# A scan and a mixture of adapters on one core: two gating subtractions bound to GpSimd, a later four-bank rotation, and one store cut into 112 and four times 4 rows

## The chip, the cores and the metric

The kernel runs on one core of a Trainium2 chip. The metric is the device time of one execution in microseconds (us), the median of several executions. A core has a TensorE (PE) for matmuls and transposes, a VectorE (DVE), a ScalarE (ACT), a GpSimd (POOL) and a SyncE (SP), each with its own instruction stream, and 16 DMA engines that move data between HBM and the on-chip memory (SBUF). Matmul results go to PSUM, which has eight banks. "PEld" in the profile is TensorE's weight load.

## The reference

```python
def _attn_ref(a, b):                       # a, b: (8, 6400, 128) float32
    h = np.zeros((B, D)); out = np.zeros_like(b)
    for t in range(S):
        h = a[:, t] * h + b[:, t]
        out[:, t] = h
    return out

def _moe_ref(x, w_gate, A, B):             # x: (51200, 128), E = 8 adapters, r = 16
    logits = x @ w_gate
    topk = np.argpartition(-logits, K, axis=1)[:, :K]        # K = 2
    sel = np.take_along_axis(logits, topk, axis=1)
    w = np.exp(sel - sel.max(-1, keepdims=True)); w /= w.sum(-1, keepdims=True) + 1e-09
    delta[mask] += w[mask, k, None] * (x[mask] @ A[e] @ B[e])   # for each adapter e, each of the two choices k
    return x + delta

def reference(**kw):
    out = _attn_ref(a, b)
    return _moe_ref(out.reshape(B * S, D), moe_w_gate, moe_A, moe_B)
```

A first-order recurrence runs along each of the 8 sequences. Its result x goes, row by row, through the two best of eight rank-16 adapters, weighted by a softmax of the two logits.

## The kernel before

**Units.** The 51,200 rows are cut into 100 units of 512 rows. For each unit w the inputs a and b are transposed on TensorE into PSUM (AB), ScalarE copies a out (aev), and VectorE runs the recurrence over the 512 columns (scan, line 520). It starts from the last column of the unit before, so the hundred scans form one chain. The result xT is float16 and lies in a ring of 16 units.

**What follows a scan.** For unit v TensorE computes the eight logits per row (L) and z = x·A for all adapters (Z). VectorE or GpSimd multiplies z by the gate weights (mul, line 739; units in POOL_MULS go to GpSimd by way of a ScalarE copy, zev, line 725). TensorE transposes the product (T), ScalarE copies it back (tev, line 796), and TensorE sums x (R) and the product times B (D) in a PSUM bank. That bank is copied into a slot of the 24-unit ring outt (oev, line 842), by ScalarE alone up to unit 89 and by ScalarE or VectorE from unit 90 on.

**Gating.** The units are put together in 29 groups, mostly of four. The last two are group 27 (units 93 to 96) and group 28 (units 97 to 99). The first three and the last two groups are "quick": VectorE sorts the eight logits of each row (mx, MAX8, line 599), then p4 (line 609) subtracts the second largest from all logits and p1 (line 618) the largest. From d2 and d1 follow p5 (line 670, a comparison), p6 (line 677, a sum), p7 (line 684, a sum) and the sigmoid on ScalarE (sig, line 694). In a quick group the planner may put each of p1, p4, p5, p6 and p7 on GpSimd or on VectorE. In the other groups they are all on GpSimd.

**Order.** A planner (`_Plan.schedule`) simulates the engines with costs in ns that are written into the source. Whenever an engine comes free it takes, of the operations that can start soonest there, the one with the smallest key. An operation that names two engines goes to the one where it can start first. The result is one fixed instruction order for each engine, with semaphore waits. All waits in an engine's stream are in that order, so whatever stands behind a waiting instruction waits too.

**PSUM banks for the sums.** Up to unit `OUT4 - 1` the sums R and D alternate between the two pO banks, and unit v waits for the copy-out of unit v-2. From unit OUT4 on four banks rotate: pO0, pO1, and the two pB banks that hold the transposed b until the last scans. There the first two units wait for the copy-outs two units back, the next two for scan 98 and scan 99, and all later ones for the copy-out four units back.

**Transfers.** All loads and stores of the big arrays are issued by SP, in the planner's order. Two units go together in one transfer of 128 rows of 4 KB. The first two and the last four units are stored alone, as 128 rows of 2 KB. `SPLIT` names stores that are issued in several pieces by rows: the pairs 66/67 and 72/73 are issued as 68 and 60 rows. Up to pair 68/69 a store also waits for the scan of a later unit (HOLD, FREE). From pair 70/71 on it waits for its copy-outs alone. The last load is issued at 160.20 us of the profiled execution, so from there on SP issues stores only.

Of the kernel before, what the change touches and what calls it, by code (L numbers as in the profile page):

```python
# [32 lines left out]
NOUT = 24  # L33
TAIL = 10
FILLS = 1
SPLIT = {66: (68, 60), 72: (68, 60)}
OUT4 = 86
LATE = {
    "sig": -205.0, "L": 9.0, "AB": -68.5, "zev": 29.9, "oev": -39.1, "tev": -12.4, "mul": -15.8, "aev": 52.7,
    "scan": 11.3, "T": 36.4, "R": 11.1,  # L40
# [60 lines left out]
class _Plan:  # L101
# [9 lines left out]
    def add(self, name, eng, kind, unit, cost, emit, deps=(), dma=None, bank=None, mode=None):  # L111

        engs = (eng,) if isinstance(eng, str) else eng
        cost = cost if isinstance(cost, dict) else {e: cost for e in engs}
        self.ops[name] = _Op(name, engs, kind, unit, cost, emit, list(deps), dma, bank, mode)
# [100 lines left out]
def bass_associative_scan_2x2__then__mixture_of_adapters_kernel(  # L216
# [18 lines left out]
    NU = N // UT  # L235
# [24 lines left out]
    with ExitStack() as stack:  # L260
# [299 lines left out]
        def gating(k):  # L560
            u0, n = groups[k]
# [3 lines left out]
            quick = k < QUICK[0] or k >= len(groups) - QUICK[1]  # L565
            ge = ("pool", "dve") if quick else "pool"
# [3 lines left out]
            def cost(t):  # L570
                p0, p1 = pool_cost[t]
                p, d = p0 + p1 * n, 160.0 + 27.0 * n
                return {"pool": (p, p + 85.0), "dve": (d - 75.0, d + 75.0)}
# [5 lines left out]
                return t[:, 0:c].to_broadcast([128, c, E])  # L579

            def step(name, eng, time, emit, deps):
                if isinstance(time, str):
                    time = cost(time)
                    time = {e: time[e] for e in ((ge,) if isinstance(ge, str) else ge)}
                add(f"{name}_{k}", eng, "gate", u, time, emit, deps)

            add(
# [14 lines left out]
            if quick:  # L602
                first, second = mx[s][:, 0:c, 0], mx[s][:, 0:c, 1]
                step("mx", "dve", (65.0 * c, 65.0 * c + 170.0), sort, [f"lev{k}", f"p1_{k - 2}", f"p4_{k - 2}"])
                step(
                    "p4",
                    ge,
# [4 lines left out]
                    [f"mx_{k}", f"p6_{k - 2}", f"p5_{k - 2}"],  # L612
                )
                step(
                    "p1",
                    ge,
# [187 lines left out]
        def o_bank(v):  # L804
            return pO[v % NO] if v < OUT4 else (pO + pB)[(v - OUT4) % 4]

        def o_free(v):
            if v < OUT4 + 2:
                return f"oev{v - NO}"
            return f"scan{NU - 2 + v % 2}" if v < OUT4 + 4 else f"oev{v - 4}"  # L810

# [49 lines left out]
        def store(j):  # L861
# [3 lines left out]
            slots = outt[:, s0 : s0 + n, :].rearrange("p n c -> p (n c)")  # L865
            sizes = SPLIT.get(u0, (128,))
            for k, size in enumerate(sizes):
# [84 lines left out]
```

## Time and profile before

| | us |
|---|---|
| median of 3 runs | 203.99 (203.7 to 204.33) |
| the profiled execution, its own time | 203.76 |
| its span, first to last instruction | 201.8 |
| TensorE busy | 190.8 (95%) |
| VectorE busy | 185.1 (92%) |
| ScalarE busy | 174.4 (86%) |
| GpSimd busy | 112.9 (56%) |
| granted TensorE clock | 0.996 |

All times inside the execution are counted from the start of the span. The profiled execution's own time is 1.96 us longer than its span, and 0.23 us shorter than the median.

How to read the profile: a row of a timeline is start, duration, engine, source line, operation, output<-input with partitions x elements, how many were merged into the row, and in square brackets the idle time before it and what ended that. A row of a table of stages gives for each engine the busy us and in brackets how many instructions fell in the stage, then the granted clock, the mean busy share of the 16 DMA engines and the GB/s they moved. A row of DMA issues gives output<-input, the issuing queue, how many, KB each, and the us from issue to landing, that is until the last of the 16 engines has finished its share. SPq is SP's queue of DMA issues.

### The profile page before, as it was taken

The page shows a single profiled execution, that of the slowest core. Times are in us where ns is not written, and L with a number is a line of the kernel's source. Part 1 is how long each engine was busy: PE and PEld are TensorE (multiplying, and loading weights), DVE is VectorE, ACT ScalarE, POOL GpSimd, SP SyncE. Part 2 cuts the span into 40 slices and gives each one's busy share as a digit, 9 for nine tenths or more (in the row PEclk, how much of TensorE's full clock was granted, in tenths as well). Part 3 has the DMA queues.
Part 4 walks back from the last instruction along what each step waited for, and adds up shares of the span by engine and source line. Part 5 has one row for each costly group of instructions (what it writes and reads, how often), then busy time and mean ns, then how long its engine had stood idle before and what let it go on. Part 6 is the DMA issues. An engine that isn't in the chain of part 4 may idle for free.

```text
span 201.8 us, 8755 instructions
## 1 busy us (share of the span) xinstructions
PE 190.8 (95%) x3594; PEld 171.3 (85%) x3594; DVE 185.1 (92%) x286; ACT 174.4 (86%) x381; POOL 112.9 (56%) x220
## 2 busy tenths in 40 slices
PE   7888989899999999999999999999999999999890
PEld 3667878798899999999999999999999998999890
DVE  1599999899999999999999999999999999999991
ACT  2367957978999999999999999999999998989991
POOL 1326577877386656746746665574675663556300
PEclk9999999999999999999999999999999999999998
DMA  6999999999999999999999999999999999998696
GB/s 180 403 409 404 410 403 406 407 403 412 406 413 413 410 413 417 409 413 411 411 411 417 409 415 410 410 415 413 409 414 413 410 413 412 411 376 338 262 374 246
DMA packets 23693, 79.35 MB, mean 393 GB/s; under 512 B 3686, under 2 KB 3814, under 8 KB 23654
## 3 DMA queue, kind: packets, MB, share of 16 engines
q1 hardware_dynamic: 22326, 78.65, 97.5%
q8 instruction: 29, 0.48, 0.9%
q10 hardware_dynamic: 1328, 0.14, 0.5%
q14 instruction: 10, 0.08, 0.1%
HBM read 52.56 MB, written 26.21 MB: 390 GB/s over the span
## 4 chain that ended last, share of the span: by engine, by line
PE 83%; DVE 8%; ACT 3%; issue 3%; POOL 1%; DVEq 0%
PE pA L95 27%; PE pO L91 21%; PE pTL L95 13%; PE pZ L91 10%; PE pTL L91 5%; DVE xT L520 5%; PE pB L95 3%; PE pB L91 3%; ACT a_st L501 2%; DVE mx L599 1%; ACT zwT L796 1%; DVE d L618 1%; ACT outt L842 1%; DVE zw L739 1%; ACT g L694 0%
## 5 line engine op out<-in xcount | busy, mean ns | idle before, releaser
L520 DVE TENSOR_TENSOR_SCAN xT<-a_st,xT,pB 128x512 f16<-128x512 f32 x96 | 120.1, 1251 | 4.1 <-ACT a_st L501 1.1
L501 ACT COPY a_st<-pA 128x512 f32<-128x512 f32 x100 | 61.0, 610 | 19.6 <-PE pB L95 15.2
L95 PE MATMUL pA<-ident_f,a_in 64*128 64x64 f32 (+1 forms) x792 | 72.1, 230 | 2.9 <-ACT a_st L501 1.9
L95 PE MATMUL pB<-ident_f,b_in 64*128 64x64 f32 (+1 forms) x792 | 72.1, 230 | 0.4 <-issue 0.2
L95 PEld LDWEIGHTS pA<-ident_f,a_in 64*128 64x128 f32 (+1 forms) x792 | 58.0, 139 | 11.6 <-ACT a_st L501 2.9
L796 ACT COPY zwT<-pTL 128x512 f16<-128x512 f16 x95 | 58.7, 618 | 0.1
L95 PEld LDWEIGHTS pB<-ident_f,b_in 64*128 64x128 f32 (+1 forms) x792 | 57.7, 139 | 1.1 <-issue 1.0
L842 ACT COPY outt<-pO 128x512 f32<-128x512 f32 x91 | 56.8, 631 | 0.7 <-PE pO L91 0.6
L739 DVE TENSOR_TENSOR zw<-pZ,g 128x512 f16<-128x512 f32 x74 | 49.9, 678 | 0.9 <-PE pZ L91 0.6
L91 PE MATMUL pO<-ident_h,xT 128*128 128x128 f16 x376 | 39.0, 227 | 0.1
L91 PE MATMUL pZ<-cst_h,xT 128*128 128x128 f16 x400 | 38.4, 219 | 0.0
L739 POOL TENSOR_TENSOR zw<-z_sb,g 128x512 f16<-128x512 f32 x26 | 27.5, 1061 | 19.3 <-PE pTL L91 17.4
L95 PE MATMUL pTL<-ident_h,zw 128*128 128x128 f16 x380 | 37.7, 222 | 0.0
L91 PE MATMUL pO<-cst_h,zwT 128*128 128x128 f16 x376 | 34.9, 217 | 0.8 <-ACT zwT L796 0.8
L91 PEld LDWEIGHTS pO<-ident_h,xT 128*128 128x128 f16 x376 | 30.9, 148 | 0.5 <-ACT outt L842 0.2
L91 PE MATMUL pTL<-cst_h,xT 128*128 128x8 f16 x400 | 27.5, 174 | 1.1 <-DVE xT L520 1.0
L91 PEld LDWEIGHTS pZ<-cst_h,xT 128*128 128x128 f16 x400 | 27.9, 114 | 0.1
L95 PEld LDWEIGHTS pTL<-ident_h,zw 128*128 128x128 f16 x380 | 21.7, 98 | 5.9
L91 PEld LDWEIGHTS pTL<-cst_h,xT 128*128 128x128 f16 x400 | 23.4, 117 | 2.4 <-DVE xT L520 1.6
L91 PEld LDWEIGHTS pO<-cst_h,zwT 128*128 128x128 f16 x376 | 22.5, 97 | 1.2 <-PE pO L91 1.0
L635 POOL TENSOR_TENSOR d<-Lg,m 128x128 f32<-128x128 f32 (+2 forms) x24 | 9.4, 391 | 21.8 <-DVE m L628 21.8
L670 POOL TENSOR_SCALAR pn<-d 128x128 f32<-128x128 f32 (+2 forms) x26 | 15.4, 593 | 2.3
(47 smaller groups left out, 149.0 us busy)
## 6 DMA issues: line engine op xcount, KB each, us to landing
a_in<-in_a_dram SPq DMA_DIRECT2D x49, 512.0 KB, 15.1
b_in<-in_b_dram SPq DMA_DIRECT2D x49, 512.0 KB, 15.0
out_dram<-outt SPq DMA_DIRECT2D x45, 512.0 KB, 15.3
out_dram<-outt SPq DMA_DIRECT2D x6, 256.0 KB, 3.2
out_dram<-outt SPq DMA_DIRECT2D x2, 272.0 KB
a_in<-in_a_dram SPq DMA_DIRECT2D x2, 256.0 KB, 9.1
b_in<-in_b_dram SPq DMA_DIRECT2D x2, 256.0 KB, 4.1
out_dram<-outt SPq DMA_DIRECT2D x2, 240.0 KB, 15.7
```

The source lines that it names most:

```text
L91: return self.h.matmul(*args, **kw)
L95: return self.h.transpose(*args)
L501: lambda h: h.copy(a_st[w % 2][:, :], pA[0][:, :]),
L520: last = h.tensor_tensor_scan(out=x_at(lo, hi), data0=a_st[w % 2][:, lo:hi], data1=pB[w % 2][:, lo:hi], initial=init, op0=ALU.mult, op1=AL ...
L599: last = h.max(mx[s][:, j, :], Lg[s][:, j, :])
L618: lambda h: h.tensor_tensor(out=v(d1[s]), in0=v(Lg[s]), in1=first.to_broadcast([128, c, E]), op=ALU.subtract),
L635: lambda h: h.tensor_tensor(out=v(d1[s]), in0=v(Lg[s]), in1=bc(m1[s]), op=ALU.subtract),
L670: lambda h: h.tensor_scalar(v(pn[s]), v(d2[s]), 0.0, -1.0e30, ALU.is_lt, ALU.mult),
L739: lambda h: h.tensor_tensor(out=oview, in0=zview, in1=gview, op=ALU.mult),
L796: lambda h: h.copy(*evacuated(v)),
L842: return copy(outt[:, v % NOUT, :], o_bank(v)[:, :])
```

## The change

```diff
-SPLIT = {66: (68, 60), 72: (68, 60)}
-OUT4 = 86
+SPLIT = {66: (68, 60), 72: (68, 60), 76: (112, 4, 4, 4, 4)}
+OUT4 = 90
+ON_G = ("p1", "p4")
...
             def step(name, eng, time, emit, deps):
+                if quick and u0 >= NU // 2 and name in ON_G:
+                    eng = "pool"
                 if isinstance(time, str):
                     time = cost(time)
-                    time = {e: time[e] for e in ((ge,) if isinstance(ge, str) else ge)}
+                    time = {e: time[e] for e in ((eng,) if isinstance(eng, str) else eng)}
                 add(f"{name}_{k}", eng, "gate", u, time, emit, deps)
```

Three things change. The store of units 76 and 77, one transfer of 128 rows, becomes five: 112 rows and four times 4 rows, each with a semaphore of its own. The rotation of four banks begins at unit 90 where it began at unit 86: units 86 to 91 alternate between the two pO banks, and units 92 and 93, no longer 88 and 89, are the ones that wait for scan 98 and scan 99. In the quick groups of the second half (27 and 28) the subtractions p1 and p4 may no longer be put on VectorE. The last changed line takes the costs of an operation for the engines that it names itself. For all other operations that is what it was. Since the planner computes every order anew, other operations near the end may change their places and engines too.

## The prediction

> **What bounds the kernel now.** I read the page's DMA lines first, then stages of the last 20 us, then the stores one by one, then the engines around the edited operations. The page:
>
> ```profile
> span 201.8 us, 8755 instructions
> PE 190.8 (95%) x3594; PEld 171.3 (85%) x3594; DVE 185.1 (92%) x286; ACT 174.4 (86%) x381; POOL 112.9 (56%) x220
> ...
> q1 hardware_dynamic: 22326, 78.65, 97.5%
> ```
>
> SP's DMA queue keeps the 16 engines 97.5% busy, so this kernel lives on its transfers. The last 18 us look different:
>
> ```profile
> 184.00:186.00 2.00, 2.00 (x31) 1.82 (x32) 2.00 (x5) 2.00 (x6) 1.74 (x2) 1.00 0.79 315
> 186.00:188.00 2.00, 1.47 (x24) 1.13 (x22) 2.00 (x5) 1.43 (x5) 0.46 (x1) 1.00 0.85 336
> 190.00:192.00 2.00, 2.00 (x39) 1.99 (x37) 2.00 (x6) 2.00 (x5) 0.96 (x3) 1.00 0.41 158
> 196.00:198.00 2.00, 0.99 (x13) 0.54 (x10) 1.21 (x2) 1.25 (x3) 0.00 (x0) 1.00 1.01 388
> 198.00:200.00 2.00, 0.00 (x0) 0.00 (x0) 0.00 (x0) 0.01 (x1) 0.00 (x0) 1.00 0.99 370
> ```
>
> Between 190 and 192 the DMA share is 0.41: most of the 16 engines have nothing to do, and the stores are late because the compute engines are. A store issued then should land soon. These are five stores of that time, pairs 78/79, 82/83, 84/85, 88/89 and the last unit, by their issue rows and, in the same order, their landings:
>
> ```profile
> 173.68 1.16 SPq L321 DMA_DIRECT2D out_dram<-outt  x1
> 180.40 0.33 SPq L321 DMA_DIRECT2D out_dram<-outt  x1
> 185.50 0.33 SPq L321 DMA_DIRECT2D out_dram<-outt  x1
> 190.73 0.33 SPq L321 DMA_DIRECT2D out_dram<-outt  x1
> 198.03 0.33 SPq L321 DMA_DIRECT2D out_dram<-outt  x1
> ...
> out_dram<-outt SPq DMA_DIRECT2D x1, 512.0 KB, 14.6
> out_dram<-outt SPq DMA_DIRECT2D x1, 512.0 KB, 10.4
> out_dram<-outt SPq DMA_DIRECT2D x1, 512.0 KB, 6.5
> out_dram<-outt SPq DMA_DIRECT2D x1, 512.0 KB, 3.8
> out_dram<-outt SPq DMA_DIRECT2D x1, 256.0 KB, 2.8
> ```
>
> Issue plus time to landing gives 188.3, 190.8, 192.0, 194.5 and 200.8. Two stores lie from the first to the second landing, one to the third, two to the fourth: 2.5, 1.2 and 2.5 us. From there three pairs and four half-size units take 6.3 us, that is 3 x 1.25 + 4 x 0.63. Whenever a store was issued, its slowest share lands 1.25 us after that of the store before. So at least one DMA engine works from 184 us to the end without a pause, with 8 rows of 4 KB per store, 1.25/8 = **0.156 us a row**. It lands at 200.8 and ends the kernel. The others wait for work.
>
> Which engine is it? The split stores tell:
>
> ```profile
> out_dram<-outt SPq DMA_DIRECT2D x1, 272.0 KB
> out_dram<-outt SPq DMA_DIRECT2D x1, 240.0 KB, 15.9
> 164.18 3.25 SPq L321 DMA_DIRECT2D out_dram<-outt  x2
> ...
> out_dram<-outt SPq DMA_DIRECT2D x1, 240.0 KB, 15.5
> 167.48 0.30 SPq L321 DMA_DIRECT2D out_dram<-outt  x1
> ```
>
> The 60-row pieces were issued at 164.60 (pair 72/73, second in the x2 row) and 167.82 (pair 66/67, right behind its 68-row piece of 167.48) and landed at 180.5 and 183.3, 2.8 us apart. An engine without a share of the 68 rows had 4 rows in between, 0.62 us. One that carries 17 of them had 21, 3.3 us. So the engine that is last at 183.3 is one that carries the 68-row pieces. The semaphore increments behind the landings, one for each engine, agree (us from the span's start, from the trace, which no view lists):
>
> ```
> pair 64/65, 128 rows   172.72 172.75 172.77 172.96 173.88 175.48 175.50 177.29 ... 179.80   (16)
> pair 72/73, 68 rows    175.28 176.50 178.12 178.34     (4, and one with the issue)
> pair 66/67, 68 rows    178.56 179.75 181.32 182.67     (4, and one with the issue)
> pair 66/67, 60 rows    ... 181.95 183.29               (15, and one with the issue)
> pair 74/75, 128 rows   174.19 ... 182.59 183.21 184.54 (16)
> last unit, 128 rows    200.21 ... 200.40 200.85        (16; 15 of them up to 200.40)
> ```
>
> 68 rows go to four engines as 17 each (173.88 + 17 x 0.156 = 176.53, shown 176.50), 60 rows to 15 as 4 each, 128 rows to 16 as 8 each. The same four take both 68-row pieces (175.28 plus 4 rows plus 17 rows, 3.28, is 178.56). From 182.67 the last time of each line follows from the one before by 4 rows and by 8 rows (0.62, 1.25).
>
> **The change part by part, the store of 76/77.** It removes 128 rows (8 for each engine) and adds 112 rows and four pieces of 4. 112 divides into 16 x 7. A piece of 4 rows is not in this trace. Cut like the 68 rows it gives one row to each of the four engines. They then get 7 + 4 = 11 rows where they had 8, +3 x 0.156 = **+0.47 us on the engine that ends the kernel**, and the twelve others -0.16. Bounds: if the small pieces went to other engines the last engine would lose a row, -0.16. If each piece cost it as much as SP needs to issue one (0.30 and 0.33 us in the rows above), 4 x 0.33 - 0.16 = +1.16. I take +0.47, since pieces of 4, 8 and 17 rows all come out at 0.156 a row, with no fixed part.
>
> [...] Were 4 rows spread evenly over all 16, it would be 0. [...]
>
> ```profile
> 169.70 3.27 SPq L321 DMA_DIRECT2D out_dram<-outt  x1
> 176.97 0.33 SPq L321 DMA_DIRECT2D out_dram<-outt  x1
> ```
>
> SP issues four more transfers behind the one at 169.70, 4 x 0.33 = 1.3 us plus what holds it as it held that one. The next stores followed at 173.68, 176.97 and 180.40, waiting for copy-outs. A delay of 1 to 2 us there reaches only engines that idle later: 0.
>
> **The subtractions.** VectorE and GpSimd around them:
>
> ```profile
> 182.99 1.26 DVE L520 TENSOR_TENSOR_SCAN xT<-a_st,xT,pB 128x512 f16<-128x512 f32 x1
> 184.17 0.64 DVE L609 TENSOR_TENSOR d<-Lg,mx 128x128 f32<-128x128 f32 x1
> 184.73 1.15 DVE L618 TENSOR_TENSOR d<-Lg,mx 128x128 f32<-128x128 f32 x1
> 185.81 0.21 DVE L670 TENSOR_SCALAR pn<-d 128x128 f32<-128x128 f32 x1
> 186.14 1.27 DVE L520 TENSOR_TENSOR_SCAN xT<-a_st,xT,pB 128x512 f16<-128x512 f32 x1
> ...
> 183.60 2.13 POOL L739 TENSOR_TENSOR zw<-z_sb,g 128x512 f16<-128x512 f32 x2 [1.09 <-ACT g L694]
> 189.50 0.37 POOL L609 TENSOR_TENSOR d<-Lg,mx 128x96 f32<-128x96 f32 x1 [2.74 <-DVE mx L599]
> ...
> L635 POOL TENSOR_TENSOR d<-Lg,m 128x128 f32<-128x128 f32 x21 | 8.5, 407 | 21.8 <-DVE m L628 21.8
> ...
> 183.83 0.66 ACT L501 COPY a_st<-pA 128x512 f32<-128x512 f32 x1
> ```
>
> Group 28's subtractions run on GpSimd already (the row at 189.50). So two instructions move, p4 and p1 of group 27: 0.64 + 1.15 = 1.79 us leave VectorE and 2 x 0.407 = 0.81 us come to GpSimd. They stand ahead of scan 99, which could start when ScalarE has copied a, at 184.49, where it started at 186.14: up to 1.65 us earlier. GpSimd idles 1.09 us ahead of its two products, so one subtraction fits there. The other goes behind the products (185.73 + 0.41 = 186.14, against 185.88 before). Then p6, p7, the sigmoid and the products of units 93 to 96 wait 0.3 us longer, or the products stand back 0.4 each. TensorE is back to back from 190 on (39 matmuls in 2 us) and has room only in 184 to 188, where 31 and 24 ran: 23 matmuls, 23 x 2/39 = 1.2 us. So the last copy-out moves by -1.2 to +0.4 us; I take -0.6. At the end it is worth **0**: the work that hides it is the last DMA engine's. Without that cover it would be worth what moves the 15 others, which finish 0.45 us before the end.
>
> [...]
>
> **The rotation from 90.** R of units 88 and 89 no longer waits for scan 98 and 99. R of 90 and 91 now waits for the copy-outs of 88 and 89 instead of 86 and 87:
>
> ```profile
> 187.47 0.30 PE L91 MATMUL pTL<-cst_h,xT 128*128 128x8 f16 x4 [0.53 <-DVE xT L520]
> 188.97 0.59 ACT L842 COPY outt<-pB 128x512 f32<-128x512 f32 x1
> 186.29 0.42 PE L91 MATMUL pO<-ident_h,xT 128*128 128x128 f16 x4
> ```
>
> R of unit 90 ran at 186.29. Copy-out 88 ended at 189.56, late only because its last sum stood behind the logits that waited for scan 99 (187.47). Bounds: 0.53 us gained, or 3.27 lost if TensorE's whole stream stood behind R90. The planner places R90 where it is free, so I take 0. Below a slip of 0.45 + 0.47 = 0.92 us it is hidden by the same engine.
>
> **Sum.** 203.76 + 0.47 + 0 + 0 = 204.23 against the profiled execution's own time. The median is 0.23 above that, so 203.99 + 0.47 = **204.46 us**.
>
> **The rivals.** *Faster:* the last engine's lateness is not a fixed cost. In the increments above it did 4 rows in 1.34 us (178.34 to 179.68 in the 60-row piece of 72/73), 0.72 too long, 0.2 more in the piece before and 0.34 in the piece after: 1.26. If that doesn't come back it ends at 200.85 + 0.47 - 1.26 = 200.06, the others at 200.40 - 0.6 = 199.8, and the kernel is 0.79 faster: 203.2. It decides once the engine is more than 0.92 earlier than I have it. Against it: three runs lie within 0.63 us, none below 203.7, where runs without the delay would show 203.5. [...]
>
> *Slower by compute:* two banks for units 86 to 91 let TensorE's stream stand behind a copy-out. A third to half of the 3.27 above, 1.5 us, puts the last store at 199.5 and the others at 201.9: +1.05, 205.0. It decides from a slip of 0.92. For it: after 190 TensorE, VectorE and ScalarE are all full. Against: VectorE gets 1.8 us back just before.
>
> *It doesn't do what it says:* the small pieces miss the last engine, -0.16, or spread, 0: 203.83 to 203.99.
>
> **How the numbers follow.** The forecast has 0.58, faster 0.18, compute 0.16, no effect 0.08. A measurement of this kernel can tell about 0.3%, 0.61 us, from no change. The forecast lies at +0.47, and its price may be as high as 1.16, so 0.30 of its 0.58 counts as slower, 0.28 as same. Slower: 0.30 + 0.16 = 0.46. Same: 0.28 + 0.07 = 0.35. Faster: 0.18 + 0.01 = 0.19. The range goes from 203.2 (the faster case) to 205.2 (the upper price, 203.99 + 1.16, which takes in the compute case). The likeliest case alone has 203.8 to 205.2.
>
> **What would show it.** Right: landings of the stores from pair 78/79 on still 1.25 us apart, each 0.47 later than 188.3, 190.8, 192.0, 194.5, however early the stores are issued; the last one over 3 us after its issue; four issues of 16 KB behind 169.7. Scan 99 before 186.14, no L609 or L618 on VectorE with 128x128, no 0.53 us wait of TensorE for the scan. Wrong: landings as before or earlier, a last store that lands within 2.4 us, or TensorE waiting for copies of pO between 186 and 192.

## The result and the profile after

| | before | after |
|---|---|---|
| median, 6 runs each (us) | 203.82 (203.29 to 204.33) | 205.25 (204.87 to 205.33) |
| profiled execution, own time | 203.76 | 205.26 |
| its span | 201.8 | 203.5 |

The changed kernel takes 1.0069 times as long, 95% interval 1.005 to 1.0088: 1.43 us more. The forecast was 0.47 more, with an upper price of 1.16, and 205.25 lies just above the forecast range, 203.2 to 205.2. The direction and the engine that pays were as forecast, the price was not. Some executions fall into a slower state (206.52 and 206.74 us of the kernel before, in the last batch): the medians of the next section hold them, the ratios leave them out.

The page of the changed kernel, span, busy times and SP's DMA queue:

```profile
span 203.5 us, 8760 instructions
PE 190.5 (94%) x3594; PEld 171.1 (84%) x3594; DVE 183.8 (90%) x284; ACT 174.7 (86%) x382; POOL 113.5 (56%) x221
...
q1 hardware_dynamic: 22342, 78.65, 97.3%
```

VectorE has 1.3 us less to do and two instructions fewer, the bytes are the same, and the span is 1.7 us longer. The same stages as in the prediction:

```profile
184.00:186.00 2.00, 2.00 (x34) 1.82 (x32) 2.00 (x4) 2.00 (x5) 1.94 (x3) 1.00 0.90 334
186.00:188.00 2.00, 2.00 (x40) 2.00 (x39) 1.79 (x5) 1.96 (x6) 0.00 (x0) 1.00 0.77 285
190.00:192.00 2.00, 2.00 (x38) 2.00 (x36) 2.00 (x5) 2.00 (x6) 0.78 (x2) 1.00 1.02 397
196.00:198.00 2.00, 0.44 (x5) 0.24 (x4) 0.00 (x0) 1.14 (x3) 0.00 (x0) 1.00 1.02 394
198.00:200.00 2.00, 0.00 (x0) 0.00 (x0) 0.00 (x0) 0.00 (x0) 0.00 (x0) 0.88 0.73 279
```

Between 184 and 188 TensorE now runs 74 matmuls where 55 ran, and from 196 on it has almost nothing left: the compute engines are ahead. The DMA engines are behind: at 190 to 192 their share is 1.02 where it was 0.41.

VectorE, GpSimd and ScalarE around the edited operations, after, and below them ScalarE's last copy-out in the kernel before:

```profile
183.02 0.43 POOL L612 TENSOR_TENSOR d<-Lg,mx 128x128 f32<-128x128 f32 x1 [0.65 <-DVE mx L602]
183.46 2.08 POOL L742 TENSOR_TENSOR zw<-z_sb,g 128x512 f16<-128x512 f32 x2
185.50 0.44 POOL L621 TENSOR_TENSOR d<-Lg,mx 128x128 f32<-128x128 f32 x1
184.03 0.58 DVE L673 TENSOR_SCALAR pn<-d 128x128 f32<-128x128 f32 x1
184.53 1.27 DVE L521 TENSOR_TENSOR_SCAN xT<-a_st,xT,pB 128x512 f16<-128x512 f32 x1
196.09 1.10 ACT L845 COPY outt<-pO 128x512 f32<-128x512 f32 x2
```

```profile
197.42 0.58 ACT L842 COPY outt<-pO 128x512 f32<-128x512 f32 x1 [0.56 <-PE pO L91]
```

Both subtractions run on GpSimd, one ahead of the two products and one behind them. Scan 99 starts at 184.53 (186.14 before), the last copy-out ends at 196.09 + 1.10 = 197.19 (198.00 before). That is the gain that was expected, and the kernel still became slower.

SP's issues of the changed kernel: the 112 rows, the four pieces of 4 rows, pair 78/79, pair 88/89 and the last unit. The second fence is the view of DMA issues, KB each and us to landing, for the 112 rows, 78/79, 88/89 and the last unit:

```profile
169.79 3.29 SPq L322 DMA_DIRECT2D out_dram<-outt  x1
173.12 1.85 SPq L322 DMA_DIRECT2D out_dram<-outt  x1
175.01 1.56 SPq L322 DMA_DIRECT2D out_dram<-outt  x1
176.62 1.64 SPq L322 DMA_DIRECT2D out_dram<-outt  x1
178.31 1.51 SPq L322 DMA_DIRECT2D out_dram<-outt  x1
179.87 1.44 SPq L322 DMA_DIRECT2D out_dram<-outt  x1
189.43 1.14 SPq L322 DMA_DIRECT2D out_dram<-outt  x1
198.27 1.03 SPq L322 DMA_DIRECT2D out_dram<-outt  x1
```

```profile
out_dram<-outt SPq DMA_DIRECT2D x1, 448.0 KB, 18.7
out_dram<-outt SPq DMA_DIRECT2D x1, 512.0 KB, 10.5
out_dram<-outt SPq DMA_DIRECT2D x1, 512.0 KB, 7.2
out_dram<-outt SPq DMA_DIRECT2D x1, 256.0 KB, 4.7
```

Issue plus time to landing is 188.5, 190.4, 196.6 and 203.0. Pair 78/79 landed at 188.3 before, 88/89 at 194.5, the last unit at 200.8: everything lands 2.1 us later, a constant delay. From 190.4 to 203.0 the 12.6 us hold eight pairs' and four units' worth of rows at the old rate (8 x 1.25 + 4 x 0.63 = 12.5). So the delay arises before 190 and is never made up. The semaphore increments date it. For a store, the last engine's landing (us from the span's start, from the trace, which no view lists):

```
                      66/67   74/75   68/69   76/77   last unit   other engines, last unit
before                183.29  184.54  185.82  187.04  200.85      15 by 200.40
after                 184.43  185.64  186.87  189.22  202.93      11 by 200.95
  in after, 76/77: 112 rows 188.48, then 4 rows each 188.66 188.85 189.04 189.22
```

The stores land in this order (68/69 goes to the queue just ahead of 76/77). All these tables, like the views, show one profiled execution of each kernel. Three parts make up 2.18 us at 76/77. The engine is 1.06 late at 68/69 already, ahead of its own pieces of the changed store. Its 11 rows then take 2.34 us where 8 took 1.22: 0.47 for three rows at 0.156, and 0.65 more, most of it in the 112 rows. Each 4-row piece costs the last engine 0.19 us, near the 0.156 of one row, with one increment on each of four engines and one with the issue, as the 68-row pieces show them. The first 4-row piece was issued at 173.12 and has its increments at 175.14 (with the issue), 183.01, 184.69, 186.04 and 188.66.

So something slowed an engine before it came to the new pieces. The other engines run up to 12 us ahead of it (the 112 rows land from 176.60 to 188.48) and came to the new pieces earlier, while it still worked on older stores. Stages of 5 us, before and then after:

```profile
175.00:180.00 5.00, 5.00 (x102) 4.60 (x100) 4.92 (x8) 4.70 (x11) 1.51 (x3) 1.00 1.01 396
180.00:185.00 5.00, 5.00 (x84) 4.64 (x82) 5.00 (x23) 4.76 (x12) 3.37 (x6) 1.00 0.89 356
```

```profile
175.00:180.00 5.00, 5.00 (x102) 4.67 (x102) 4.92 (x9) 4.70 (x10) 1.52 (x3) 1.00 0.91 351
180.00:185.00 5.00, 5.00 (x84) 4.60 (x81) 5.00 (x22) 4.76 (x12) 3.94 (x7) 1.00 0.88 291
```

From 180 to 185 the engines are as busy as before (0.88 and 0.89) and move 291 GB/s, not 356. Their packets take longer. The mean of the 4 KB packets that begin in that stage is 197 ns after and 162 ns before (the longest 1129 and 491 ns; 351 and 434 packets).

### The profile page after: what moved, and what is told of

The parts are those of the page before. It is cut to its first block, busy times and chain, and to the rows that moved or that the text cites. A ratio compares the mean times of both kernels' runs of the same rounds, so it can differ in the third digit from the quotient of the medians.

```text
span 203.5 us, 8760 instructions
## 1 busy us (share of the span) xinstructions
PE 190.5 (94%) x3594; PEld 171.1 (84%) x3594; DVE 183.8 (90%) x284; ACT 174.7 (86%) x382; POOL 113.5 (56%) x221
## 4 chain that ended last, share of the span: by engine, by line
PE 87%; DVE 4%; ACT 3%; issue 2%; POOL 1%
PE pA L96 28%; PE pO L92 23%; PE pTL L96 14%; PE pZ L92 10%; PE pTL L92 5%; PE pB L96 3%; DVE xT L521 2%; PE pB L92 2%; ACT a_st L502 1%; ACT outt L845 1%; DVE mx L602 1%; ACT zwT L799 1%; DVE zw L742 0%; ACT g L697 0%; ACT Lg L596 0%
## 5 line engine op out<-in xcount | busy, mean ns | idle before, releaser
L845 ACT COPY outt<-pO 128x512 f32<-128x512 f32 x94 | 58.2, 628 | 0.2
L92 PE MATMUL pO<-cst_h,zwT 128*128 128x128 f16 x384 | 35.5, 218 | 0.8 <-ACT zwT L799 0.7
L92 PEld LDWEIGHTS pO<-ident_h,xT 128*128 128x128 f16 x384 | 31.4, 147 | 0.5 <-ACT outt L845 0.2
```

The source lines that it names most:

```text
L92: return self.h.matmul(*args, **kw)
L845: return copy(outt[:, v % NOUT, :], o_bank(v)[:, :])
```

## The experiments

Each ran beside the kernel before on the same chip, in up to five rounds. The batches are: the first four, the next four, the next three, then one, then three. The letter of a theory holds within its batch.

| edit | median (us) | before | ratio, 95% interval |
|---|---|---|---|
| store alone (112, 4, 4, 4, 4) | 205.20 | 203.73 | 1.0083 (1.0057 to 1.0109) |
| change without the store | 203.58 | 203.73 | 0.9995 (0.9983 to 1.0006) |
| store 64, 16, 16, 16, 16 | 204.84 | 203.73 | 1.0054 (1.0032 to 1.0077) |
| no split stores at all | 204.25 | 203.73 | 1.0038 (1.001 to 1.0066) |
| store 112, 16 | 204.81 | 203.69 | 1.0065 (1.0038 to 1.0092) |
| four pairs as two transfers of one unit | 203.32 | 203.69 | 0.9997 (0.9973 to 1.0021) |
| 112, 4, 4, 4, 4 at pair 90/91 instead | 204.30 | 203.69 | 1.0036 (1.001 to 1.0061) |
| change, only pair 66/67 split | 203.57 | 203.69 | 0.9995 (0.9985 to 1.0006) |
| 112, 16 at pair 90/91 | 204.03 | 203.68 | 1.0025 (1.0002 to 1.0048) |
| change, old splits moved to 82/83, 84/85 | 204.50 | 203.68 | 1.0029 (1.001 to 1.0049) |
| before, old splits moved there | 204.21 | 203.68 | 1.0008 (0.9986 to 1.0029) |
| store 64, 64 | 205.25 | 203.60 | 1.0075 (1.0056 to 1.0093) |
| change with 64, 64 | 205.18 | 203.74 | 1.0065 (1.0041 to 1.0088) |
| change with 112, 16 | 204.68 | 203.74 | 1.0050 (1.0032 to 1.0068) |
| change without its store, half stores | 203.47 | 203.74 | 0.9977 (0.9959 to 0.9994) |

### Which part of the change

The store alone, on the kernel before:

```diff
-SPLIT = {66: (68, 60), 72: (68, 60)}
+SPLIT = {66: (68, 60), 72: (68, 60), 76: (112, 4, 4, 4, 4)}
```

> The kernel before with the store of 76/77 as 112 and four times 4 rows, and nothing else. Theory A (the store loads the four DMA engines that end the kernel): the whole loss, +1.0 to +1.6 us against before, slowest landings behind 76/77 later than in before by 1.0 or more and 1.25 us apart to the end. Theory B (the new order of the compute engines costs it): within 0.3 us of before.

The rest alone, with the store whole:

```diff
-OUT4 = 86
+OUT4 = 90
+ON_G = ("p1", "p4")
...
+                if quick and u0 >= NU // 2 and name in ON_G:
+                    eng = "pool"
```

> The kernel after with the store of 76/77 in one piece of 128 rows, as before; the subtractions on GpSimd and the rotation from unit 90 stay. Theory A: between 0.5 us faster than before and 0.2 slower, since the last DMA engine has the work it had, and the compute engines end earlier. Theory B: +1.0 to +1.6 us.

Measured: +1.47 us for the store alone, -0.15 for the rest, which can't be told from no change. The whole loss is the store's. With the store alone the compute engines are not late: ScalarE's last copy-out ends at 197.97 (198.00 before), and the last unit lands 2.11 us later.

```profile
197.39 0.58 ACT L842 COPY outt<-pO 128x512 f32<-128x512 f32 x1 [0.56 <-PE pO L91]
```

The end of the kernel without the store, ScalarE's last copies and the last unit's issue and landing:

```profile
196.59 1.10 ACT L845 COPY outt<-pO 128x512 f32<-128x512 f32 x2
197.72 0.33 SPq L322 DMA_DIRECT2D out_dram<-outt  x1
```

```profile
out_dram<-outt SPq DMA_DIRECT2D x1, 256.0 KB, 2.9
```

The copies end 0.31 us earlier than before, at 197.69, and the last unit lands at 200.6 (200.60 by the increments, 200.85 before). Of the other engines 14 have landed it by 199.92 there, where 15 had by 200.40 before. The gain of the compute engines ends in front of the last DMA engine.

### What of the store: rows, issues or shape

Five issues, but with eight rows for each engine:

```diff
+SPLIT = {66: (68, 60), 72: (68, 60), 76: (64, 16, 16, 16, 16)}
```

> The kernel before with the store of 76/77 as 64 and four times 16 rows: five issues as in after, but each DMA engine gets 4 + 4 x 1 = 8 rows, as with one piece. Theory A in its plain form (only rows on the last engine count): within 0.3 us of before. Theory C (SP is held up by more issues, and the stores behind come late): SP's issues behind it last 1 us and more as in after, and +0.8 us or more.

Two pieces, seven rows and one row for each engine:

```diff
+SPLIT = {66: (68, 60), 72: (68, 60), 76: (112, 16)}
```

> The kernel before with the store of 76/77 as 112 and 16 rows: 7 + 1 = 8 rows for each engine and one issue more. Theory A (only rows on the last engine count): within 0.3 us of before. Theory C (SP's issues): at most +0.3. Theory D (a piece that is not 128 rows slows the packets of all engines that move at the same time): +0.5 to +1.2, and the store of 68/69, issued ahead of it, lands 0.6 us or more later than in before.

More issues, every one of them 128 rows high: the pairs 68/69, 74/75, 76/77 and 78/79 each as two transfers of one unit, rows of 2 KB:

```diff
+HALF = (68, 74, 76, 78)
...
+            if u0 in HALF:
+                for k in range(2):
+                    part = slice(k * UT, (k + 1) * UT)
+                    add_dma(f"st{j}p{k}" if k else f"st{j}", "sp", u0 + HOLD, [(rows[:, part], slots[:, part])],
...
```

> The kernel before with the stores of pairs 68, 74, 76 and 78 issued unit by unit, each as two transfers of 128 rows of 2 KB: four more issues at the place where after has four more, all of 128 rows, the same bytes on every engine. Theory C: +0.8 us or more. Theories A and D: within 0.3 us of before.

Measured: +1.11 and +1.12 us for the two in which no engine moves a row more than before (by an even division, an estimate from the 16 increments that 128 and 112 rows show), -0.37 by medians and a ratio of 0.9997 (0.9973 to 1.0021) for the one with four more issues. With 112 and 16 rows the store of 68/69, ahead of them in the queue, lands 0.95 us later than before, as theory D said. So most of the loss comes neither from more rows on an engine nor from the number of issues. The stage from 180 to 185 us with 112 and 16 rows, and with the half stores:

```profile
180.00:185.00 5.00, 4.31 (x74) 3.93 (x72) 5.00 (x23) 4.24 (x11) 2.26 (x5) 1.00 0.92 304
```

```profile
180.00:185.00 5.00, 5.00 (x85) 4.60 (x82) 5.00 (x22) 4.76 (x12) 3.53 (x6) 1.00 0.90 336
```

The first moves 304/0.92 = 330 GB/s for a full share of the engines, as after (291/0.88 = 331), the second 336/0.90 = 373, with packets of half the size. Before it was 356/0.89 = 400. Of what was varied here, a piece that is not 128 rows high is what slows the engines.

The plainest such piece, two halves on the kernel before:

```diff
+SPLIT = {66: (68, 60), 72: (68, 60), 76: (64, 64)}
```

> The kernel before with the store of units 76 and 77 as two pieces of 64 rows, four rows on each of the 16 engines per piece, so that every engine moves as many rows as before, in two pieces of the same shape. Theory A (any piece that is not 128 rows high takes its rows from other partitions than a whole store does, and the packets of the engines that move at that moment get longer): 0.6 to 1.3 us slower than before, like the piece pair 112 and 16 (+1.1 us). Theory B (only small pieces cost, with one row for each engine, or pieces that give seven rows): within 0.35 us of before. By A the stretch from 175 to 185 us of the trace moves fewer bytes for each busy share of the engines than in before; by B as many.

Measured: +1.65 us by the medians and 1.53 by the ratio, above the range expected by theory A. Its profiled execution took 208.5 us, far from the median, and shows something else, in the stage from 185 to 190 (granted clock 0.69) and in TensorE's waits (us in total, times, longest):

```profile
185.00:190.00 5.00, 4.09 (x42) 3.75 (x42) 2.29 (x11) 2.94 (x6) 1.06 (x1) 0.69 0.66 247
```

```profile
PE pO L91 <- issue: 2.4, 1, 2.4
```

TensorE stood still for 2.4 us on its own issue, with no wait for another engine shown. With 112 and 16 rows it did so for 0.7, and ScalarE's last copy-out ended at 198.96, 0.96 later than before. With 64 and four times 16 rows it ended at 198.57, with no such wait. So part of these losses might have come through TensorE or another compute engine. Two further runs have the changed compute order, which is 0.3 to 0.8 us ahead and would cover part of such a stop, and a third repeats the half stores under it:

```diff
-SPLIT = {66: (68, 60), 72: (68, 60), 76: (112, 4, 4, 4, 4)}
+SPLIT = {66: (68, 60), 72: (68, 60), 76: (64, 64)}
```

> The changed order of the compute engines (both subtractions on GpSimd, rotation from unit 90), with the store of units 76 and 77 as two pieces of 64 rows. Every engine moves as many rows as with one store of 128; the compute engines end some 0.8 us earlier than in before. Theory A (pieces that are not 128 rows high make the packets of all engines in motion longer, and the last DMA engine pays): 0.7 to 1.5 us slower than before; in the trace the last landing is 0.8 us or more behind the others, and the stretch from 180 to 185 us moves about 300 GB/s. Theory C (the pieces delay the transfer that brings TensorE its code, TensorE stands still and the last copies come late): slower too, but all 16 engines finish the last store together, within 0.3 us, and TensorE shows a wait for its own issue of over 0.5 us.

```diff
+SPLIT = {66: (68, 60), 72: (68, 60), 76: (112, 16)}
```

> The same with the store of units 76 and 77 as 112 and 16 rows, seven rows and one row for each engine: the change without the three more rows on the four engines. Theory A: 0.6 to 1.2 us slower than before, with the last engine landing 0.6 us or more behind the others, and 0.3 to 0.7 us faster than the changed kernel, by the three rows. Theory C: TensorE shows a wait for its own issue, and all 16 engines finish the last store together.

```diff
+SPLIT = {66: (68, 60), 72: (68, 60)}
+HALF = (68, 74, 76, 78)
```

> The changed order of the compute engines, the store of units 76 and 77 whole by rows, and four stores (units 68/69, 74/75, 76/77, 78/79) issued as two transfers each, one for each unit, 128 rows of 2 KB. Theory A: as many issues as in the change and no piece of another height than 128, so no slower than before: -0.5 to +0.2 us. If the number of issues cost the time, it would be 0.7 us or more slower.

Measured: +1.44, +0.94 and -0.27 us. With 64 and 64 the trace shows no wait of TensorE for its issue after 150 us. ScalarE's last copies and the last unit's issue and landing:

```profile
196.15 1.10 ACT L845 COPY outt<-pO 128x512 f32<-128x512 f32 x2
197.56 1.04 SPq L322 DMA_DIRECT2D out_dram<-outt  x1
```

```profile
out_dram<-outt SPq DMA_DIRECT2D x1, 256.0 KB, 5.9
```

It lands at 203.5, 2.65 us later than before, though it was issued 0.47 earlier. Thirteen engines are through at 200.28. That is theory A: the last DMA engine pays, not TensorE. (This execution took 206.22 us, the longest of its seven, so 2.65 is more than a usual one would show.) With 112 and 16 rows TensorE waits 0.7 us for its issue again:

```profile
PE pO L92 <- issue: 0.7, 1, 0.7
```

Yet the other 15 engines finish at 200.86 and the last at 201.72, so there too the engine ends it. The landings in the same terms as above (the half stores in pairs):

```
                      66/67   74/75   68/69   76/77   last unit   other engines, last unit
without the store     182.82  184.05  185.31  186.55  200.60      14 by 199.92
store alone           184.28  185.47  186.72  189.20  202.96      14 by 201.35
112, 16               184.28  185.53  186.77  188.68  202.45      14 by 201.36
change with 112, 16   183.64  184.88  186.13  187.94  201.72      15 by 200.86
change with 64, 64    185.98  187.19  188.43  189.69  203.50      13 by 200.28
half stores           183.37  184.63  185.91  187.19  201.13      14 by 200.23
```

With pieces of other heights the last engine is late at 66/67 already, three stores ahead of 76/77. With half stores it is within 0.15 us of the kernel before at every pair, and its last unit lands 0.28 later, which the time does not show. The change itself has three rows more on four engines, and three issues more, than its version with 112 and 16 rows: 1.43 - 0.94 = 0.49 us by medians, while the two intervals overlap (1.005 to 1.0088, 1.0032 to 1.0068). With the half stores the changed order is the only version below before with its whole interval, 0.06 to 0.41% faster; its middle, 0.23%, is within the 0.3% that the prediction called no change.

### Where the place counts

The same pieces at pair 90/91, where most engines wait for work:

```diff
+SPLIT = {66: (68, 60), 72: (68, 60), 90: (112, 4, 4, 4, 4)}
```

> The kernel before with the pieces 112, 4, 4, 4, 4 for the store of 90/91 in place of 76/77, issued at about 191.7 us, when most DMA engines have nothing to do. The four engines get the same 3 rows more. Theory A: +0.45 to +0.75 us and no more. Theory D: the same, since there is little beside it to slow down; if the pieces cost their whole price at any place, +1.2 us or more.

```diff
+SPLIT = {66: (68, 60), 72: (68, 60), 90: (112, 16)}
```

> The kernel before with the store of units 90 and 91 as 112 rows and 16 rows, issued when 15 of the 16 DMA engines have little left to move. Every engine still gets eight rows of that store, so no engine moves more bytes than before. Theory A (a piece that is not 128 rows high slows the packets of the other engines that move at that moment, and so costs only while they are busy): within 0.35 us of the kernel before. Theory B (such a piece costs the engine that carries it some 1 us wherever it stands): 0.8 to 1.2 us slower than before, as the same split of units 76 and 77 was. The difference to the run with four pieces of 4 rows at this place (+0.61 us) is the price of the three rows more: 0.3 to 0.6 us by A.

Measured: +0.61 and +0.35 us, under half of what the same pieces cost at 76/77. The difference points to the three rows, but the two intervals overlap widely (1.001 to 1.0061, 1.0002 to 1.0048). The slowing moves with the pieces. The stage from 190 to 195 us of the two kernels and of before:

```profile
190.00:195.00 5.00, 5.00 (x90) 4.99 (x89) 5.00 (x10) 4.88 (x11) 1.25 (x4) 1.00 0.68 239
```

```profile
190.00:195.00 5.00, 5.00 (x91) 4.99 (x89) 5.00 (x10) 4.86 (x11) 1.33 (x4) 1.00 0.72 256
```

```profile
190.00:195.00 5.00, 5.00 (x92) 4.99 (x89) 5.00 (x11) 4.87 (x12) 0.96 (x3) 1.00 0.77 306
```

The mean 4 KB packet of that stage takes 182 and 183 ns, 164 before, and from 180 to 185 us it has its old 164 and 165. That it costs less there would fit engines that wait for work (their share in this stage was 0.77 before, from 180 to 185 us 0.89), but no run separates this from other causes. The second lies at the upper end of what theory A allowed. What the time is lost to at this place the profiles don't show: all 16 engines finish the last unit within 0.5 us of each other, by 201.40 and 200.81, and the profiled executions, 203.74 and 203.51, are no slower than the kernel before.

### The splits that were there already

```diff
-SPLIT = {66: (68, 60), 72: (68, 60)}
+SPLIT = {}
```

> The kernel before with no split store at all. Theory A: the four engines lose 2 x (17 + 4 - 8) = 26 rows, 4.1 us, and are no longer last; another engine gets 8 rows more than in before and ends it, and the time is between 0.6 us faster and 0.3 slower than before. If the splits of 66/67 and 72/73 are needed to level the engines: slower by more than 0.6.

```diff
-SPLIT = {66: (68, 60), 72: (68, 60), 76: (112, 4, 4, 4, 4)}
+SPLIT = {66: (68, 60)}
```

> The kernel after with the subtractions on GpSimd and the rotation from 90, the store of 76/77 whole and only 66/67 split. The engines of the 68 rows lose 13 rows, 2.0 us, and are no longer last. Theory A and D: 0.3 to 0.8 us faster than before, the last store landing within 2.6 us of its issue. If the two splits are both needed: slower than before.

```diff
+SPLIT = {82: (68, 60), 84: (68, 60)}
```

> The changed order of the compute engines (both subtractions on GpSimd, the rotation from unit 90), the store of units 76 and 77 whole, and the two stores in 68 and 60 rows moved from units 66 and 72 to 82 and 84. Theory A: the 68-row pieces fall where the other engines have little left to move, and the engine that is behind carries no row of the 60-row pieces as before: 0.4 to 1.0 us faster than before. Theory B: the place of a split does not matter, only its rows: within 0.3 us of the kernel with the compute order changed and the store whole (-0.1 us).

> The kernel before with its two split stores moved from units 66 and 72 to 82 and 84, and nothing else. Theory A: 0.2 to 0.8 us faster than before, and the same place gives 0.2 to 0.4 us more with the changed compute order, whose last copies end earlier. Theory B: within 0.3 us of before.

Measured: +0.52 without splits, -0.12 with one and the changed order, +0.82 with the two splits moved and the changed order, +0.53 with them moved in the kernel before (ratio 1.0008, not told from no change). Without splits, which came out between what the two theories allowed, a single engine lands the last unit 0.93 us behind the 15 others, at 201.56. So the old splits, odd as their heights are, earn their place by taking rows from an engine that falls behind. One may be enough: with the changed order one split took 203.57 and two took 203.58, where 0.3 to 0.8 us less than before was expected of the one. Moving them was a miss too: I had taken 82/83 and 84/85 for places where the engines wait. From 185 to 190 us the kernel with them moved and the changed order shows

```profile
185.00:190.00 5.00, 5.00 (x83) 4.68 (x82) 4.79 (x20) 4.96 (x12) 1.65 (x3) 1.00 0.79 270
```

at 190 ns for the mean 4 KB packet (163 before). The engines were still moving there, and paid.

## Why the prediction was right and wrong

**What bounds the kernel.** Right. In the kernels before and after, the last engine works without a pause (from 78/79 on its pairs land 1.21 to 1.33 us apart before, 1.23 to 1.27 after) and the end follows it: the compute engines' lead (0.31 us without the store) was worth 0.15, not told from nothing. Only with the pieces at 90/91 (within 0.5 us), and in the long execution with 64 and 64 (the last unit landed 2.4 us after its issue), do all 16 engines end together.

**The store: the step that failed.** The prediction took "+0.47, since pieces of 4, 8 and 17 rows all come out at 0.156 a row, with no fixed part". The term for the rows was about right, as far as the runs tell: the change and its version with 112 and 16 rows differ by 0.49 us, the store alone and its version by 0.35, with intervals that overlap, and a 4-row piece took 0.19 us on the engine that ends the kernel. What the sum lacked is a price that no row count shows. With equal rows on every engine, pieces that are not 128 rows high still cost 0.94 (112 and 16) and 1.44 us (64 and 64) under the changed order, while the engines moved 351 and 342 GB/s for a full share from 180 to 185 us (316/0.90 and 328/0.96), where it was 400 before. The 0.94 and the 0.49 make up the 1.43 measured because the one was taken off to get the other. The upper bound of 1.16 was built from four issues of SP. It lay near for the wrong reason.

The evidence stood in the prediction's own increments: the last engine did four rows in 1.34 us while the 68- and 60-row pieces of 72/73 and 66/67 were under way. The prediction priced that lateness of 1.26 us as one which might not come back, in the faster rival. Read as a price of odd pieces it would have spoken for slower. The traces bear out part of each reading. From 175 to 180 us the mean 4 KB packet takes 166 ns in the kernel before and 161 in the three kernels with no split there (none at all, or both moved). But between the landings of the two 68-row pieces the last of their engines has 21 rows, and with the same two splits these took 4.33 us before, 3.42 without the store, 3.92 with half stores and 3.60 with 112 and 16 rows at 90/91, so up to 0.9 us of it comes and goes. How much is the price of the pieces stays open.

**SP's delay.** Forecast 1 to 2 us at 78/79. It was 6.2 (179.87 against 173.68), as each 4-row issue took 1.5 to 1.85 us, not 0.33. It was worth nothing in the time, as forecast: the half stores hold SP up as long (78/79 at 178.34 and 180.39) and cost nothing that can be told. Behind the last engine the delay can be seen: with the store alone the last unit is issued 0.62 us later than before, and 14 engines finish it at 201.35.

**The subtractions.** Right in every step: scan 99 was 1.61 us earlier (up to 1.65), the last copy-out 0.81 (0.6 taken), and together with the rotation that was worth 0 at the end. The comparison p5 took 0.58 us beside GpSimd's products (183.46 to 185.54), where before it took 0.21, begun at 185.81 behind their end at 185.73. It ended at 184.61, behind the first product (184.53) and not behind both (185.54), so it cost 0.37 us more and not the gain of scan 99. Why it took longer there no view shows.

**The rotation.** Forecast 0. TensorE shows no wait between 184 and 192 us in the changed kernel, so neither the 0.53 of before nor the 3.27 feared. The slower rival by compute did not happen.

**From the engine to the time.** The last landing moved by 2.08 us, the profiled time by 1.50. Behind the last landing the span goes on for 0.9 us before and 0.5 after, which takes back 0.4. The other 0.2 is the time outside the span (1.96 and 1.76). The stretch behind the landing is 0.5 to 0.6 us in the profiles with four or more additional issues and 0.9 in those with fewer, so it also hides the 0.28 of the half stores. Why was not tried.

## What to carry to other kernels

When a store is cut into pieces by rows, price not only the rows that each engine gets but also what the pieces do to the transfers beside them. Here a store in pieces that were not 128 rows high cost 0.9 to 1.5 us where the engines were busy, with equal rows on every engine, and as many issues at full height, cut along the columns, cost nothing that the time shows. A slow stretch that the trace of before shows beside an operation of the kind to be added deserves a term of its own in the sum, or a run, before it is put down to chance.

## What the runs showed of the hardware

- Beside pieces of another height than 128 rows the transfers were slower: the mean 4 KB packet took 197 ns instead of 162 from 180 to 185 us, single ones up to 1129 ns (491 before), and the last engine fell 1.06 us behind before it came to its own pieces. Whether an engine that gets no row of such a piece is slowed too is not shown: the 112 rows lie on all 16 (16 increments from 176.60 to 188.48). No run here shows in which order the engines take the rows or separates the on-chip side from the HBM side, so the cause stays open.
- SP's issues stayed slow in the changed kernel: 1.03 us for the last one (0.33 before), long after the pieces of 4 rows. The half stores with the changed order show 1.02 for theirs, and lose nothing that the time shows.
- TensorE stood still on its own issue for 0.7 us in both kernels with 112 and 16 rows at 76/77, and for 2.4 in the execution of 208.5 us with 64 and 64, but not in the changed kernel. What it waits for there is not shown.
